# A new opening list, up to the eighth input unit, in a fused kernel of clustered attention and a SiLU expert

## The chip, the cores and the metric

One Trainium2 chip, one core of it. The metric is the time of one execution of the whole kernel on the device, in microseconds; lower is better. Before and after are compared as medians of several executions.

## What is computed

Attention over 4 batches, 8 heads, 768 positions and 64 dimensions. Each query and each key belongs to the one of 16 cluster centres of its head to which its normalised vector is closest, and a query sees only keys of its own cluster. A feed-forward layer with SiLU follows on all 3072 tokens (512 to 2048 to 512).

```python
q_assign = np.argmax(np.einsum('bhsd,hcd->bhsc', q_n, c_n), axis=-1)
k_assign = np.argmax(np.einsum('bhsd,hcd->bhsc', k_n, c_n), axis=-1)
mask = q_assign[:, :, :, None] == k_assign[:, :, None, :]
scores = np.where(mask, scale * np.matmul(q, k.transpose(0, 1, 3, 2)), -1e9)
attn = np.exp(scores - scores.max(-1, keepdims=True))
x = np.matmul(attn / attn.sum(-1, keepdims=True), v)      # (B, H, S, D) -> (B*S, H*D)
h = x @ w_in
return (h * (1.0 / (1.0 + np.exp(-h)))) @ w_out
```

## The kernel before

A **job** brings the queries and keys of one head from memory to the form in which they are multiplied. `load` fetches float32 rows, `hi` and `lo` split them into two float16 halves (scaled by 128), a transpose turns them into `ab` tiles with the 64 dimensions on partitions: on TensorE (`tr`, with `ev` to copy the result out of its bank) in the opening, by DMA (`xpose`) later. `logits_n` multiplies the tiles with the normalised centres (`stk`), `mx_n` and `ge_n` on VectorE make a one-hot code of the largest, and the code is written into 16 further partitions of the same `ab` tile. A match of codes then adds the same large number to a score, so that the exponential of a score without a match vanishes.

The code gets there by one of two ways. With `ct_mm`, `ct_q` and `ct_k`, nine transposes on TensorE put it where it belongs in a bank, and one ScalarE and two VectorE copies bring it from there into `ab`. With `cd_mm` and `cd_ev`, two matmuls and one copy make a tile `cd`, and a DMA on SP's queue moves it. Jobs of batches 2 and 3 use a DMA transpose and a move on GpSimd's queue.

For the first batch, jobs `k0` to `k7` hold a head's keys and the first half of its queries, and jobs `x0` and `x1` the second half of the queries of four heads each. Jobs `h8` to `h31` are the later batches' heads.

Work on TensorE comes in units. There are 192 **score units** (`qk_mm`: two matmuls of 384 columns for one half of the queries of a head and two key blocks), three for each head and half: units 0 to 23 are the first half of batch 0, units 24 to 35 the second half of its heads 0 to 3, which need `x0`'s codes. `exp` on ScalarE turns each into a tile `P`. Two banks hold scores, so score u waits for exp u-2. `pv` multiplies a pair of heads' `P` with the values (36 matmuls of 65 columns), `norm` divides by the row sums on VectorE, and `xn_t` with `xn_ev`, or the DMA transpose `xn_d`, turn the result into `xt`. An **input unit** (`unit_a`, 4 matmuls of 384 columns) multiplies `xt` with 128 columns of `w_in`; tanh on ScalarE and the gate on VectorE follow. An **output part** (`part_b`, 4 matmuls of 512 columns) multiplies with `w_out`.

Four further banks (0 to 3) hold everything else; an operation of the opening names its banks.

The order of work is fixed in the program in two ways. The **opening** is a list written out by hand or by a search (`plan`, line 650): each word is an operation with its index, an engine letter (A, D, P) or its banks, and each engine takes its own pieces in the order of the list. Words: `hi`/`lo`/`tr`/`ev` as above, `L` logits, `mx`, `ge`, `cm` and `ce` for `cd_mm` and `cd_ev`, `ct`, `ctq`, `ctk`; `x...` the same for jobs x0 and x1; `vl` and `v` load and cast values, `w` loads expert weights (0 to 3 and 4 to 7 are the two halves of `w_in`), `qk`, `ex`, `pa` `pb` `pc` or `px` `py` the parts of a `pv`, `nm`, `pt`, `pe` its normalisation, transpose and eviction; `a` and `e` begin and end an input unit; `r` loads a later job; `j` is filler work on TensorE.

Behind the list, from line 678, a **scheduler** in the program orders everything else: it keeps a model clock of each engine (lengths in us, such as 0.325 for a score unit), lets each engine take the piece that is ready with the best rank, and for TensorE (`options`, line 850) a score unit goes first when it is due (`PACE0`, `PACE`, line 859). Steps of a job get dates in score units (`p`, line 778), and `lanes` holds each engine's pieces with a lateness that orders them (`add`, line 694). None of this runs on the chip; it only decides the order in which instructions are issued. The list ends with unit 24 scored and three input units (`FIRST`, line 682; `range(3)`, line 793).

Of the kernel before, what the change touches and what calls it, by code (L numbers as in the profile page):

```python
# [28 lines left out]
@with_exitstack  # L29
def kernel(  # L30
# [10 lines left out]
    nc = tc.nc  # L41
# [118 lines left out]
    def logits_n(job, bk=None, w=HC, ns=None):  # L160
        ab = abs_[job.name]
        if job.name not in psNs:
            psNs[job.name] = bank("psN", n=bk)
        psN = psNs[job.name]
        m = (job.n + 1) // 2
        L = psN[:, 0 : 2 * w * m].rearrange("p (h c m) -> p h c m", h=2, m=m)
        for n in ns or range(2 * m):
            i = min(n, job.n - 1)
            for x in range(0, 2 * HC, w):
                nc.tensor.matmul(  # L170
                    L[:, n % 2, :, n // 2], ab[:, i, :], stk[:, job.groups[i // 3][0], x : x + w],
                    start=(x == 0), stop=(x + w == 2 * HC),
                )
        Ls[job.name] = L

# [3 lines left out]
    def lsum(job, last=True):  # L179
        m, P = job.n // 2, Ls[job.name]  # L180
        L = mp.tile([128, 2, HC, 6], f32, name="L", bufs=2)
        nc.vector.tensor_reduce(  # L182
            out=L[:, :, :, 0:m], in_=P.rearrange("p h (n c) m -> p h c m n", n=2), axis=AX.X, op=ALU.add
        )
        if last:
            done(psNs.pop(job.name))
        Ls[job.name] = L[:, :, :, 0:m]

    def ohv(job):
        m = (job.n + 1) // 2  # L190
        if job.late:
            return ohd[nn[job.name] % 3][:, :, 0 : HC * m].rearrange("p h (c m) -> p h c m", m=m)
        return ohm[nn[job.name] % 3][:, 0 : 2 * HC * m].rearrange("p (h c m) -> p h c m", h=2, m=m)

    def mx_n(job):
        m = (job.n + 1) // 2
        mx = mxn[job.name] = mp.tile([128, 12], f32, name="mxn", bufs=3)
        nc.vector.tensor_reduce(
            out=mx[:, 0 : 2 * m].rearrange("p (h m) -> p h m", h=2), in_=Ls[job.name].rearrange("p h c m -> p h m c"),
            axis=AX.X, op=ALU.max,  # L200
        )

    def ge_n(job):
        m = (job.n + 1) // 2
        nn[job.name] = len(nn)
        mx = mxn.pop(job.name)[:, 0 : 2 * m].rearrange("p (h m) -> p h m", h=2)
        nc.vector.tensor_tensor(  # L207
            out=ohv(job), in0=Ls.pop(job.name), in1=mx.unsqueeze(2).to_broadcast([128, 2, HC, m]), op=ALU.is_ge
        )
# [43 lines left out]
    def ct_mm(job, banks):  # L253
        for part, lo_, n, bk in (("q", 6, 3, banks[0]), ("k", 0, 6, banks[1])):
            pC = psCs[job.name, part] = bank("pC", f16, bk)
            for m in range(lo_, lo_ + n):
                x = 128 * (m - lo_)
                nc.tensor.transpose(pC[64 : 64 + HC, x : x + 128], ohv(job)[:, m % 2, :, m // 2], ident)
        psNs.pop(job.name)
# [297 lines left out]
    def first(op, n, eng, banks):  # L557
# [22 lines left out]
        elif op == "L":  # L580
            logits_n(job, banks[0])
        elif op == "mx":
# [79 lines left out]
    """.split()  # L662
    for word in plan:
        name, *rest = word.split(".")
# [16 lines left out]
    free.append(3)  # L681
    FIRST = 24
    PACE0, PACE = 1.3, 1.40
    HOLD = 6
# [27 lines left out]
    def date(s, f):  # L712
        dates.setdefault(s, []).append(f)

    code_at, tensor_todo = {}, []

    def chain(job, b):
# [7 lines left out]
        def turned(t):  # L725
            add("SP", t, 1.65, lambda: xpose(job), lambda t: tensor_todo.append((lands(t, 2.45) + (5.0 if b == 3 else 2.2 if b == 2 else 1.8), 0.35, lambda: logits_1(job), sums)))

# [48 lines left out]
    for i in range(H, B * H):  # L776
        b, h = divmod(i, H)
        p = int((32 + 3.2 * h, 64+5.2*h, 106+5.2*h)[b - 1]) | 1
        job = jobs[i]
        if i > H + 3:  # L780
            date(max(FIRST, p - (8 + min(h, 4) if b == 1 else 12)), lambda t, job=job: add("SP", t, 1.25, lambda: load(job), lambda t: got(job, t)))
        if i >= H + 2:
# [6 lines left out]

    exp_at = {u: 0.0 for u in range(FIRST - 1)}  # L790
    exp_at[FIRST - 1] = 0.0
    exp_at[FIRST] = 0.9
    x_at, gate_at = {}, {(0, 0, fb): 0.0 for fb in range(3)}
    pv_next = 4
    qa, qb = [(0, 0, fb) for fb in range(3, NFB)], []
    x_at[0, 0] = 0.0
    turn, po_on = 0, None
    unit = FIRST + 1

    def by_dma(n):  # L800
        return 8 <= n < 8 * B - 1

    def norm_piece(n, t):
        b, c, i = n // 8, n // 4 % 2, n // 8 * H + 2 * (n % 4)

        def ready(t):
            if n % 4 == 3:
                x_at[b, c] = t
                if n < 8 * B - 1:
# [40 lines left out]
    def options(t):  # L850
# [26 lines left out]
    def tensor_piece(o):  # L877
        nonlocal unit, pv_next, turn
        rank, r, length, what = o
        if what == "qk":  # L880
# [124 lines left out]
```

## Time and profile before

| | |
|---|---|
| median of 3 runs | 305.55 us (304.91 to 306.67) |
| the profiled execution | 306.13 us |
| its span | 304.4 us |
| TensorE busy | 297.6 us, 98% of the span |
| ScalarE busy | 213.3 us |
| VectorE busy | 202.1 us |
| GpSimd busy | 70.4 us |
| moved by DMA | 44.00 MB |

The span is the time between the first and the last event of the profiled execution. The page's slices give each engine's busy share in 40 equal parts of the span (7.6 us each), in tenths. A busy time is a union of the intervals in which an instruction is under way: short matmuls overlap each other, and so a stretch can count as busy although more would fit into it. In the lines of groups the columns are: source line, engine, operation, what is written from what, shapes, count; then busy us and the mean ns of one; then idle time of the engine ahead of them.

### The profile page before, as it was taken

What the parts mean: (1) busy time and instruction counts of PE and PEld (TensorE: products, weight loads), DVE (VectorE), ACT (ScalarE), POOL (GpSimd) and SP (SyncE); (2) the same over time, 40 slices, a digit from 0 to 9 for tenths busy, and PEclk for the clock granted to TensorE, in tenths of its full rate; (3) what the DMA queues carried; (4) which work ended last, traced back from release to release, by engine and by line L of the source; (5) the groups of instructions that cost most, each with busy time, mean ns of one, the idle gap of its engine ahead of it and who ended that gap; (6) DMA issues with size and microseconds to landing.
All of it is one profiled execution on the core that took longest, in us unless ns stands there. A gap on an engine that the chain in (4) does not pass through costs nothing.

```text
span 304.4 us, 7844 instructions
## 1 busy us (share of the span) xinstructions
PE 297.6 (98%) x3152; PEld 188.2 (62%) x3152; DVE 202.1 (66%) x431; ACT 213.3 (70%) x344; POOL 70.4 (23%) x130
## 2 busy tenths in 40 slices
PE   7899999999999999999999999999999999999996
PEld 3777856666666566665666566656665566655544
DVE  5997759888997669966679548873553235424542
ACT  5899979665887569965787658966996569752420
POOL 2987510111310332353222243212100000000000
PEclk9999999999999999999999999999999999999999
DMA  6989899999975799687998978552101110011012
GB/s 212 245 215 204 137 254 233 198 293 216 246 141 129 169 239 169 159 188 173 209 212 143 250 170 167 127 116 71 28 16 47 53 66 15 15 47 57 14 60 78
DMA packets 74419, 44.00 MB, mean 145 GB/s; under 512 B 54704, under 2 KB 69392, under 8 KB 74384
## 3 DMA queue, kind: packets, MB, share of 16 engines
q1 hardware_dynamic: 69296, 35.09, 49.1%
q0 software_dynamic: 4800, 8.13, 14.5%
q8 instruction: 24, 0.39, 0.5%
q10 hardware_dynamic: 288, 0.30, 0.3%
q14 instruction: 11, 0.09, 0.1%
HBM read 27.30 MB, written 6.29 MB: 110 GB/s over the span
## 4 chain that ended last, share of the span: by engine, by line
PE 87%; DMA 5%; ACT 3%; DVE 3%; issue 1%; SPq 1%; DVEq 0%
PE po L463 26%; PE ph L405 24%; PE pS L338 19%; PE pO L355 10%; PE psN L170 3%; DMA ab<-cd 2%; ACT P L343 2%; PE phs L443 2%; DMA raw<-in_k_dram 1%; PE po L969 1%; DMA vn<-in_v_dram 1%; DVE hl L122 1%; SPq L102 1%; PE pTk L145 0%; ACT ab L262 0%
## 5 line engine op out<-in xcount | busy, mean ns | idle before, releaser
L343 ACT ACTIVATE P<-pS 128x768 f16<-128x768 f32 x192 | 153.5, 816 | 53.4 <-PE pS L338 53.1
L338 PE MATMUL pS<-ab 128*128 128x384 f16 x384 | 91.4, 326 | 0.7 <-DMA ab<-cd 0.3
L405 PE MATMUL ph<-xt,win_s 128*128 128x384 f16 x480 | 91.0, 326 | 0.3 <-DVE gt L428 0.3
L463 PE MATMUL po<-wout_s,gt 128*128 128x512 f16 x368 | 91.0, 379 | 0.0
L428 DVE SCALAR_TENSOR_TENSOR gt<-tn,ph 128x384 f16<-128x384 f32 x120 | 63.0, 550 | 22.5 <-ACT tn L425 21.7
L425 ACT ACTIVATE tn<-ph 128x384 f32<-128x384 f32 x120 | 58.7, 504 | 9.8 <-PE ph L405 8.6
L405 PEld LDWEIGHTS <-win_s 128*128 128x128 f16 x480 | 46.1, 98 | 30.2 <-issue 0.9
L463 PEld LDWEIGHTS <-gt 128*128 128x128 f16 x368 | 35.4, 98 | 34.6
L338 PEld LDWEIGHTS <-ab 128*128 128x128 f16 x384 | 34.5, 98 | 26.3 <-issue 1.6
L355 PEld LDWEIGHTS <-P 128*128 128x128 f16 x1152 | 39.4, 97 | 4.0
L355 PE MATMUL pO<-vt,P 128*128 128x65 f16 x1152 | 41.0, 193 | 0.0
L470 DVE TENSOR_SCALAR ot<-po 128x512 f32<-128x512 f32 x23 | 15.9, 690 | 31.6 <-PE po L463 31.5
L122 DVE SCALAR_TENSOR_TENSOR hl<-raw,hl 128x768 f16<-128x768 f32 (+3 forms) x35 | 32.3, 926 | 0.9 <-ACT hl L113 0.3
L285 POOL CAST vt<-vn 128x384 f16<-128x384 f32 x32 | 17.6, 554 | 43.7 <-DMA vn<-in_v_dram 40.4
L227 POOL DMA_DIRECT2D ab<-cdt x16 | 9.1, 566 | 55.1 <-PE pS L338 19.4
L170 PEld LDWEIGHTS <-ab 128*128 128x128 f16 x472 | 17.4, 97 | 4.1
L182 DVE TENSOR_REDUCE L<-psN 128x192 f32<-128x384 f32 x26 | 14.3, 551 | 7.0 <-PE psN L170 6.9
L214 POOL TENSOR_SCALAR od<-od 128x96 f16<-128x96 f16 x16 | 9.8, 615 | 38.7 <-DVE od L207 38.6
L367 DVE TENSOR_TENSOR xn<-pO,zr 128x384 f16<-128x384 f32 x32 | 17.8, 558 | 1.1
L365 DVE RECIPROCAL zr<-pO 128x6 f32<-128x6 f32 x32 | 6.2, 193 | 18.6 <-PE pO L355 18.4
L170 PE MATMUL psN<-stk,ab 128*128 128x32 f16 (+1 forms) x472 | 18.4, 187 | 0.0
L117 DVE TENSOR_SCALAR hl<-raw 128x768 f16<-128x768 f32 x24 | 13.6, 567 | 0.7 <-DMA raw<-in_k_dram 0.7
(75 smaller groups left out, 162.9 us busy)
## 6 DMA issues: line engine op xcount, KB each, us to landing
raw<-in_k_dram SPq DMA_DIRECT2D x31, 192.0 KB, 3.7
out_dram<-ot SPq DMA_DIRECT2D x23, 256.0 KB, 2.2
raw<-in_q_dram SPq DMA_DIRECT2D x24, 192.0 KB, 3.6
vn<-in_v_dram SPq DMA_DIRECT2D x16, 192.0 KB, 4.4
vn<-in_v_dram POOLq DMA_DIRECT2D x16, 192.0 KB, 3.5
win_s<-in_moe_w_in_dram POOLq DMA_DIRECT2D x8, 256.0 KB, 6.3
wout_s<-in_moe_w_out_dram POOLq DMA_DIRECT2D x4, 512.0 KB, 10.6
raw<-in_q_dram SPq DMA_DIRECT2D x2, 384.0 KB, 5.0
```

The costliest lines, as they stand in the source:

```text
L122: nc.vector.scalar_tensor_tensor(out=hl[:, s, 1, :], in0=raws[job.name][:, s, :], scalar=QS, in1=hl[:, s, 0, :], op0=ALU.mult, op1=ALU.sub ...
L170: nc.tensor.matmul(L[:, n % 2, :, n // 2], ab[:, i, :], stk[:, job.groups[i // 3][0], x : x + w], start=(x == 0), stop=(x + w == 2 * HC),)
L285: nc.gpsimd.tensor_copy(vt[:, :, 0:D], vns.pop(i))
L338: nc.tensor.matmul(pS[:, e, 0:HALF], abs_[kj.name][:, kn, :], rhs, start=True, stop=True)
L343: nc.scalar.activation(out=P, in_=pst.pop(u)[:, :, 0:HALF], func=AF.Exp, bias=0.0, scale=ESC)
L355: nc.tensor.matmul(o[:, (2 * t + h) * VW : (2 * t + h + 1) * VW], Ps[i + h, c, j // 2][:, j % 2, ts(t, 128)], vtb[(i + h) % 13][:, j, 0:VW ...
L367: nc.vector.tensor_tensor(out=xn, in0=ov[:, :, 0:D], in1=zr.unsqueeze(2).to_broadcast([128, 2 * NM, D]), op=ALU.mult)
L405: nc.tensor.matmul(ph[:, 0:HALF], win_s[:, r, ts(fb, 128)], xts[b, c][:, r, :], start=(r == 0), stop=(r == NR - 1))
L425: nc.scalar.activation(out=tn, in_=ph[:, 0:HALF], func=AF.Tanh, bias=0.0, scale=0.5)
L428: nc.vector.scalar_tensor_tensor(out=gt[:, fb, :], in0=tn, scalar=1.0, in1=ph[:, 0:HALF], op0=ALU.add, op1=ALU.mult)
L463: nc.tensor.matmul(po, gts[b, c][:, fc, ts(t, 128)], wout_s[:, fc, :], start=(fc == 0), stop=(fc == NFB - 1))
L470: nc.vector.tensor_scalar(out=ot, in0=po, scalar1=0.5, scalar2=None, op0=ALU.mult)
```

## The change

A new list takes the place of the old one. It scores units 0 to 26 (before 0 to 24) and holds eight input units (before three); at its end stand the ends of two of them and six whole ones, with only one exponential and loads between. Heads 0 and 3 get their codes by `ct` (before heads 0, 1, 3, 4, 6 and 7), heads 1, 2, 4, 5, 6 and 7 by `cm` and `ce` (before heads 2 and 5). GpSimd splits four of the heads (3, 5, 7, 6; before 3, 5, 7). Jobs with `ct` use a flat layout (`flat`: nine code columns in one row, not two halves of five), so their logits are nine tiles and not ten. Head 7's logits are made 32 wide and summed by `ls`; the other heads' stay 16 wide in two accumulating matmuls.

In the scheduler, the number of scores and input units in the list is counted (`listed_s`, `listed_e`); the pace of the score units follows the stock of input and output work instead of a fixed pace; pair 11 is transposed by TensorE instead of by DMA; the dates of batch 2 move slightly; DMA loads get a lateness of 3, and so does the DMA transpose of batches 2 and 3.

```diff
@@ class Job @@
+        self.halves, self.m = 2, (self.n + 1) // 2
+    def flat(self):
+        self.halves, self.m = 1, self.n
...
@@ logits_n @@
-        m = (job.n + 1) // 2
-        L = psN[:, 0 : 2 * w * m].rearrange("p (h c m) -> p h c m", h=2, m=m)
-        for n in ns or range(2 * m):
+        g, m = job.halves, job.m
+        L = psN[:, 0 : g * w * m].rearrange("p (h c m) -> p h c m", h=g, m=m)
+        for n in ns or range(g * m):
...
@@ first @@
         elif op == "L":
-            logits_n(job, banks[0])
+            logits_n(job, banks[0], 2 * HC if eng else HC)
+        elif op == "ls":
+            lsum(job, False)
...
     plan = """
-        hk0 hq0 lk0 hi1.A cn0 j3.0 c5.01 lq0 hi2.A vl1 stk tk0.2 xr0 kad tq0.3 lo1 evq0.A hi3.P evk0.D tr1.01 evq1.A
-        hi4.A lo2 L0.2 evk1.D mx0 ge0 tr2.31 lo3 evq2.A ct0.02 ctk0 L1.1 lo4 evk2.A L2.3 ctq0 hi6.A tr3.02 evk3.D mx1
-        evq3.A qk0 mx2 ge1 ge2 qk1 w0 tr4.02 evq4.D ex0 qk2 cm2 hi5.P ct1.12 lo5 evk4.A ce2.A L3.0 ctq1 w1 hi7.P ex1
-        xh0.P vl0 ctk1 tr5.31 v1 ex2 qk3 mx3 evk5.D ge3 xr1 evq5.D L4.2 vl3 qk4 ex3 lo6 ct3.30 ex4 mx4 qk5 ctq3 L5.1
-        v0 ex5 ctk3 w2 mx5 vl2 ge5 ge4 qk6 tr6.30 qk7 evk6.D cm5 w3 vl5 w4 ce5.D xh1.P ex6 vl7 qk8 xl0 evq6.A ex7 ex8
-        ct4.23 pa0.0 ctq4 qk9 L6.1 w5 ex9 qk10 pb0 vl4 qk11 v3 pc0 ex10 lo7 ctk4 tr7.23 ex11 evq7.A qk12 ex12 mx6 qk13
-        ge6 nm0 v5 evk7.D pt0.0 ct6.13 qk14 xp0.2 xl1 pe0.A ex13 xu0.D ex14 ctk6 L7.0 qk15 w6 ctq6 xp1.2 qk16 mx7
-        xq0.3 ge7 v2 ex15 xu1.D ex16 ct7.10 qk17 xw0.D xL0.2 xM0 vl6 xs0 qk18 pa1.3 ex17 pb1 xm0 ex18 ctk7 v4 ctq7
-        qk19 qk20 pc1 w7 ex19 xg0 pa2.1 xc0 qk21 xq1.0 v7 ex20 qk22 ex21 xw1.A pb2 v6 xe0.D pc2 vl9 nm1 xL1.2 qk23 xM1
-        nm2 xs1 pt1.3 xm1 px3.0 xg1 ex22 ex23 pt2.1 vl8 w8 py3 w9 r8 pe1.A pe2.A w10 xc1 r9 nm3 a0.3 xe1.D w11 pt3.1
-        a1.0 r10 pe3.D e1 e0 e2.2 qk24 ex24 r11
+        hk0 hq0 hi1.A lk0 cn0 lq0 lo1 tk0.0 hi2.A evk0.D j3.1 c5.12 kad tq0.3 lo2 evq0.A tr1.23 stk vl4 L0.0 vl0
+        evq1.A evk1.D mx0 ge0 hi4.A tr2.13 evq2.A L1.2 hi3.P ct0.03 lo4 mx1 ge1 xr0 cm1 ctk0 hi5.P evk2.A lo5 ctq0
+        tr4.10 ce1.A qk0 hi7.P evk4.A lo3 L2.3 evq4.A tr5.21 mx2 evk5.D ge2 qk1 ex0 qk2 evq5.A w0 lo7 L4.0 vl1 ex1 mx4
+        cm2 tr3.12 ex2 ce2.A xr1 qk3 evq3.D evk3.A qk4 hi6.P tr7.32 ge4 lo6 cm4 L3.1 evq7.D xh0.P ex3 qk5 vl2 evk7.D
+        ce4.A v4 mx3 w1 ex4 tr6.20 evk6.D ex5 L5.3 ge3 mx5 vl5 qk6 v1 evq6.A ct3.21 vl3 ge5 qk7 cm5 L6.0 xl0 ctk3 ex6
+        ctq3 qk8 ce5.A L7.S.2 xq0.3 mx6 ge6 w2 ls7 xp0.1 xw0.D v0 xh1.P ex7 cm6 v2 v5 qk9 ex8 ce6.A qk10 ex9 pa0.3 mx7
+        ge7 pb0 vl6 xu0.D xl1 qk11 xL0.0 ex10 cm7 vl7 qk12 v3 ex11 xM0 ce7.D xs0 w3 pc0 v7 qk13 r8 xp1.1 ex12 qk14 xm0
+        ex13 xu1.D ex14 w4 xq1.2 qk15 xg0 v6 nm0 pa1.1 qk16 xw1.D xc0 pt0.3 ex15 xe0.D ex16 qk17 ex17 xL1.2 w5 pb1
+        qk18 vl8 ex18 xM1 qk19 pe0.D pc1 qk20 nm1 vl9 xs1 pa2.0 ex19 ex20 qk21 pb2 qk22 ex21 pc2 xm1 xg1 ex22 nm2 w6
+        qk23 px3.3 pt1.1 pe1.D ex23 pt2.0 xc1 py3 qk24 pe2.D w7 r9 xe1.A r10 nm3 ex24 qk25 a0.1 pt3.0 w8 qk26 a1.2
+        pe3.D ex25 w9 e0 e1 w10 e6.3 r11 e4.0 ex26 e2.1 e3.2 e5.3 w11 e7.0
     """.split()
+    for word in plan:
+        if word[:2] == "ct" and word[2].isdigit():
+            jobs[int(word[2])].flat()
+    listed_e = sum(w[0] == "e" and w[1].isdigit() for w in plan)
+    listed_s = sum(w[:2] == "ex" for w in plan)
...
-    FIRST = 24
-    PACE0, PACE = 1.3, 1.40
+    FIRST = listed_s
+    PACE, LEAST, GAIN = 1.40, 12, .03
...
-        p = int((32 + 3.2 * h, 64+5.2*h, 106+5.2*h)[b - 1]) | 1
+        p = int((32 + 3.2 * h, 67+5.0*h, 106+5.2*h)[b - 1]) | 1
...
     def by_dma(n):
-        return 8 <= n < 8 * B - 1
+        return 8 <= n < 8 * B - 1 and n != 11
...
@@ options @@
-                due = t >= PACE0 * min(unit - FIRST - 1, 24) + PACE * max(unit - FIRST - 25, 0)
+                stock = 1.302 * len(qa) + 0.863 * len(qb) + 20.8 * (unit // 24 - released)
+                due = t >= scored + min(max(PACE + GAIN * (stock - LEAST - 0.867 * (24 - unit % 24)), 0.8), 2.2)
...
@@ tensor_piece, behind a score unit @@
+            scored = max(clock["PE"] - 0.325, scored + 0.8)
```

More of the change, by code (lines that the diff above doesn't have):

```diff
@@ L170, in logits_n @@
                 nc.tensor.matmul(
-                    L[:, n % 2, :, n // 2], ab[:, i, :], stk[:, job.groups[i // 3][0], x : x + w],
+                    L[:, n % g, :, n // g], ab[:, i, :], stk[:, job.groups[i // 3][0], x : x + w],
                     start=(x == 0), stop=(x + w == 2 * HC),
@@ L179, in lsum @@
     def lsum(job, last=True):
-        m, P = job.n // 2, Ls[job.name]
-        L = mp.tile([128, 2, HC, 6], f32, name="L", bufs=2)
+        g, m, P = job.halves, job.m, Ls[job.name]
+        L = mp.tile([128, 12 * HC], f32, name="L", bufs=2)[:, 0 : g * HC * m].rearrange("p (h c m) -> p h c m", h=g, m=m)
         nc.vector.tensor_reduce(
-            out=L[:, :, :, 0:m], in_=P.rearrange("p h (n c) m -> p h c m n", n=2), axis=AX.X, op=ALU.add
+            out=L, in_=P.rearrange("p h (n c) m -> p h c m n", n=2), axis=AX.X, op=ALU.add
         )
@@ L257, in ct_mm @@
                 x = 128 * (m - lo_)
-                nc.tensor.transpose(pC[64 : 64 + HC, x : x + 128], ohv(job)[:, m % 2, :, m // 2], ident)
+                nc.tensor.transpose(pC[64 : 64 + HC, x : x + 128], ohv(job)[:, m % job.halves, :, m // job.halves], ident)
         psNs.pop(job.name)
@@ L712, in date @@
     def date(s, f):
[L713 removed]
+        dates.setdefault(max(s, FIRST), []).append(f)
     code_at, tensor_todo = {}, []
@@ L787 @@
         date(60, lambda t, od=od: add("POOL", t, 0.3, lambda: nc.gpsimd.memset(od, 0.0)))
[L790 to L793, printed above, removed]
+    exp_at = {u: 0.0 for u in range(FIRST)}
+    exp_at[FIRST - 1] = 0.9
+    x_at, gate_at = {}, {(0, 0, fb): 0.0 for fb in range(listed_e)}
     pv_next = 4
-    qa, qb = [(0, 0, fb) for fb in range(3, NFB)], []
+    qa, qb = [(0, 0, fb) for fb in range(listed_e, NFB)], []
     x_at[0, 0] = 0.0
     turn, po_on = 0, None
-    unit = FIRST + 1
+    released, scored = 1, -1.0
+    unit = FIRST
     def by_dma(n):
-        return 8 <= n < 8 * B - 1
+        return 8 <= n < 8 * B - 1 and n != 11
     def norm_piece(n, t):
@@ L806, in ready @@
         def ready(t):
+            nonlocal released
             if n % 4 == 3:
+                released += 1
                 x_at[b, c] = t
@@ L877, in tensor_piece @@
     def tensor_piece(o):
-        nonlocal unit, pv_next, turn
+        nonlocal unit, pv_next, turn, scored
         rank, r, length, what = o
```

20 lines of the change are left out of this document (10 added, 10 removed).

## The prediction

> **What bounds the kernel now.** The profiled execution took 306.13 us in all with a span of 304.4, so 1.73 us lie around the span; the median of the three runs is 305.55, or 0.58 below the profiled one. I read the page's busy times and slices first, then TensorE by stretches.
>
> ```profile
> PE 297.6 (98%) x3152; PEld 188.2 (62%) x3152; DVE 202.1 (66%) x431; ACT 213.3 (70%) x344; POOL 70.4 (23%) x130
> ...
> PE   7899999999999999999999999999999999999996
> ...
> PEclk9999999999999999999999999999999999999999
> ...
> 41.00:291.00 250.00, 249.50 (x2497) 155.26 (x2496) 165.33 (x330) 179.30 (x288) 45.44 (x91) 1.00 0.63 139
> ```
>
> The reader is to see that TensorE is the bound from 41 us on: 249.50 busy of 250.00 at a granted clock of 1.00. Nothing is to be had there but by giving TensorE fewer instructions. The busy share flatters the opening, because a short matmul counts with its whole latency. So I work with pitches, the distance at which equal matmuls follow each other, from the order of time on TensorE:
>
> ```profile
> 10.28 1.17 PE L170 MATMUL psN<-stk,ab 128*128 128x16 f16 x40
> 11.29 0.49 PE L145 MATMUL pTk<-ident,hl 128*128 128x128 f16 x6
> ...
> 11.90 0.81 PE L338 MATMUL pS<-ab 128*128 128x384 f16 x4
> ...
> 17.47 0.68 PE L258 MATMUL pC<-ident,om 128*16 128x128 f16 x9
> 18.08 0.50 PE L338 MATMUL pS<-ab 128*128 128x384 f16 x2
> ...
> 30.13 0.51 PE L170 MATMUL psN<-stk,ab 128*128 128x32 f16 x12
> 30.48 0.49 PE L338 MATMUL pS<-ab 128*128 128x384 f16 x2
> ...
> 35.16 0.49 PE L338 MATMUL pS<-ab 128*128 128x384 f16 x2
> ...
> 40.48 0.81 PE L338 MATMUL pS<-ab 128*128 128x384 f16 x4 [0.32 <-DMA ab<-cd]
> ...
> 43.72 1.46 PE L405 MATMUL ph<-xt,win_s 128*128 128x384 f16 x8
> 45.02 0.49 PE L338 MATMUL pS<-ab 128*128 128x384 f16 x2
> ...
> 48.11 1.09 PE pO L355 x36
> ```
>
> The first two numbers of a line are its start and length. Pitches: a 16-wide logit 1.01/40 = 0.025 us, a 32-wide one 0.35/12 = 0.029, an input matmul 1.30/8 = 0.1625, the same for a score matmul (equal width), a value matmul 1.09/36 = 0.030 (last line, from the chain of waits). For transposes I take the length less one matmul's own 0.22 us: (0.49 - 0.22)/5 = 0.054 for a tile, (0.68 - 0.22)/8 = 0.0575 for a code tile (0.61/9 = 0.068 if the gap behind counts too).
>
> The starts give a milestone that both kernels pass with the same work done: eight input units finished and score units 0 to 27 issued. Counting score pairs, unit 0 starts at 11.90, unit 23 at 35.16, unit 28 at 45.02. **So the milestone of before is 45.02 us**, and the question is when the new list gets there.
>
> **The change part by part.** First the matmul count, by the order of the built programs against these groups:
>
> ```profile
> L170 PE MATMUL psN<-stk,ab 128*128 128x32 f16 x312 | 13.3, 193 | 0.0
> L170 PE MATMUL psN<-stk,ab 128*128 128x16 f16 x160 | 5.1, 176 | 0.0
> L258 PE MATMUL pC<-ident,om 128*16 128x128 f16 x54 | 4.1, 221 | 0.4 <-DVE om L207 0.4
> L236 PE MATMUL psN<-ident,om 128*80 128x128 f16 x4 | 0.6, 226 | 0.0
> ```
>
> Code transposes go from 54 to 18 (-36 x 0.0575 = -2.07 us), the code matmuls of heads from 4 to 12 (+8 x 0.054 = +0.43), 16-wide logits from 160 to 136 (-0.60), 32-wide ones from 312 to 322 (+0.29), transposes of normalised outputs from 27 to 30 (+0.16, since pair 11 no longer goes by DMA). Sum -1.8 us. All but the last lie ahead of the milestone. They are worth 1.8 only if TensorE is what the opening waits for, and until unit 23 it isn't: ScalarE is.
>
> ```profile
> 12.49 0.81 ACT L343 ACTIVATE P<-pS 128x768 f16<-128x768 f32 x1
> 13.63 0.81 ACT L154 ACTIVATE ab<-pTk 128x768 f16<-128x768 f16 x1 [0.34 <-PE pTk L145]
> 14.37 0.47 ACT L247 ACTIVATE cd<-psN,kadd 80x256 f16<-80x256 f32 x1
> 14.86 0.48 ACT L262 ACTIVATE ab<-pC 16x384 f16<-16x384 f16 x1
> 15.37 3.02 ACT L343 ACTIVATE P<-pS 128x768 f16<-128x768 f32 x4
> ...
> 20.31 0.50 ACT L154 ACTIVATE ab<-pTq 128x384 f16<-128x384 f16 x1
> 20.68 1.53 ACT L343 ACTIVATE P<-pS 128x768 f16<-128x768 f32 x2
> ...
> 35.15 1.54 ACT L343 ACTIVATE P<-pS 128x768 f16<-128x768 f32 x2
> ```
>
> From start to start: an exponential 3.02/4 = 0.755, a K eviction 0.74, a code copy out of the bank 0.49, a query code copy 0.51, a Q eviction 0.37. Before, exp 0 starts at 12.49 and exp 22 at 35.15, which is 22.66 us: 22 exponentials (16.61) and between them one K eviction (0.74), one bank copy (0.49), five query code copies (2.55), two Q evictions (0.74), and two pieces that the new list gives to VectorE, x1's 768-wide Q eviction and the first output pair's, taken like head evictions of their widths (0.74 + 0.37): together 22.24. ScalarE idled only about 0.4.
>
> *The start of the exponentials.* The new list puts head 1's maximum and comparison ahead of head 0's key codes on VectorE, and head 1's bank copy, head 4's K and Q evictions ahead of exp 0 on ScalarE:
>
> ```profile
> 8.94 0.31 DVE L198 TENSOR_REDUCE mxn<-psN 128x10 f32<-128x160 f32 x1
> 9.28 0.33 DVE L207 TENSOR_TENSOR om<-psN,mxn 128x160 f16<-128x160 f32 x1
> ...
> 11.04 0.62 DVE L269 TENSOR_SCALAR ab<-pC 16x256 f16<-16x256 f16 x2
> ```
>
> Key codes follow at 11.04 + 0.31 + 0.33, so unit 0 is scored near 11.90 + 0.6 = 12.5. On ScalarE the bank copy waits for that comparison and a short code matmul (11.7 + 0.3 = 12.0), ends at 12.5, then come 0.74 and 0.37 for head 4 with about 0.1 of hand-over: exp 0 at 13.7, 1.2 us later than before.
>
> *The stream behind it.* Until exp 22 the new order has on ScalarE 16.61 of exponentials, two Q evictions (0.74), one K eviction (0.74), four bank copies (1.96) and one query code copy (0.51): 20.56. With the same idle 0.4, exp 22 starts at 13.7 + 21.0 = 34.7, 0.45 earlier than before, and with it score unit 23.
>
> *From unit 23 to the milestone.* Now TensorE has work queued without a gap: five score units (10 x 0.1625), 32 input matmuls (5.2), 36 value matmuls (1.09), nine transposes (0.49), two code matmuls (0.11): 8.5 us, which ends at 43.2. Before, the same plus six logits (0.17) is 8.7 us and took 9.86; 1.2 us went into waits, one of them the 0.32 for x0's codes at 40.48. The new list has x0's code copy five scores earlier and only the last pair's transpose and eviction close to the input units, covered by units 25 and 26. I take no loss here; the bounds are 0 and the 1.2 of before.
>
> *What is added: waits for code transfers.* Heads 1, 4, 6 and 7 now send their codes through a DMA on SP's queue instead of copies on ScalarE and VectorE, as heads 2 and 5 did. Before shows these four in the opening, those of heads 2 and 5, x0 and x1: the issues of the first two and then each landing (us, last column), in order of time, with the stretches' DMA share (last but one column):
>
> ```profile
> 14.86 0.69 SPq L251 DMA_DIRECT2D ab<-cd  x1
> ...
> 20.92 0.58 SPq L251 DMA_DIRECT2D ab<-cd  x1
> ```
> ```profile
> ab<-cd SPq DMA_DIRECT2D x1, 40.0 KB, 2.6
> ...
> ab<-cd SPq DMA_DIRECT2D x1, 40.0 KB, 6.7
> ...
> ab<-cd SPq DMA_DIRECT2D x1, 48.0 KB, 6.7
> ...
> ab<-cd SPq DMA_DIRECT2D x1, 48.0 KB, 10.5
> ```
> ```profile
> 12.00:16.00 4.00, 3.62 (x57) 2.61 (x55) 3.86 (x12) 3.51 (x6) 3.44 (x2) 1.00 0.83 145
> 16.00:20.00 4.00, 3.82 (x69) 2.89 (x68) 3.67 (x11) 3.95 (x7) 3.04 (x6) 1.00 0.78 241
> 20.00:24.00 4.00, 3.85 (x68) 2.77 (x67) 3.70 (x9) 3.95 (x7) 3.56 (x2) 1.00 1.16 196
> ```
>
> The tightest is head 2. Its bank copy follows exp 2: 13.7 + 3 x 0.755 + 0.37 + 0.49 = 16.8, and the issue comes at once. Exp 6 could start at 16.8 + 0.74 + 0.755 + 0.49 + 1.51 + 0.37 = 20.7, so unit 6 wants the codes by 20.15. A landing in 2.6 us costs nothing, one in 6.7 lands at 23.5 and costs 3.4. The issue is two us behind the 2.6 row and four ahead of the 6.7 one, so I go a third of the way: 4.0 us, a wait of 0.7. Queued behind the waiting score on TensorE are later heads' logits and transposes, so ScalarE, VectorE and the later code copies all move with it; later heads then have their slack enlarged and I charge them nothing more. Head 1, issued near 12.5 and wanted near 17, is safe up to 4.5 us.
>
> By the Trainium skill, "DMA: Bandwidth & Descriptors", section on the anatomy of one DMA, a transfer costs about 2.0 us plus its bytes over 436e3 per us (fitted there on the GpSimd path), an estimate of 2.1 for 40 KB. By that no code is late and the sum is the first rival below. The trace agrees only where the DMA share was 0.83 (2.6); at 1.16 it shows 6.7.
>
> *GpSimd* takes one more split (head 6) and sends the expert weights later; the weights' second half is first wanted behind the milestone, so I put this at nothing, covered by the eight first-half input units.
>
> **Sum.** Milestone 43.2 + 0.7 = 43.9 against 45.02: -1.1. Behind it the two programs have equal counts but for the three transposes, +0.16. The new pacing rule and dates only permute that work: from a job's logits to the first score that uses it the shortest stretch holds 9.8 us of TensorE work against 10.1 before, and from the last pair of batch 1's first half to its first input unit 2.4. Before lost 0.5 in that stage; I take the same. So -0.95 against the profiled time, and against the median 305.55 - 0.95 = **304.6 us**.
>
> **The rivals.** (1) *All codes land in time*: milestone 43.2, -1.8 + 0.16, 303.9 us. For it the 2.6 row, against it the 6.7 one. (2) *Slower: x0's codes come late at unit 24.* Its copy is listed ahead of exp 16, which ScalarE reaches near 29.7; I put the issue at 30. Unit 24 stands on TensorE behind the last value matmuls, near 36.95, and every input unit of the list stands behind it. With 6.7 the codes land at 36.7 and cost nothing; with the 10.5 that x1's took, they land at 40.5 and all stops for 3.55 us. With head 2's 0.7 that makes a milestone of 47.4, +2.4 + 0.16, or about 308.1 us; alone it is 307.4. It decides from a landing of about 9 us on. For it: the list loads batch 1's data ahead of that transfer. Against: 6.7 in the comparable place. (3) *The opening's gain is given back in the rest*, by the new pace letting ScalarE or a bank run late by 1 us or so: 305.6. Against it, the distances above.
>
> **How the numbers follow.** Forecast 0.4, (1) 0.3, (2) 0.2, (3) 0.1. What a measurement can tell from no change is about 0.5%, 1.5 us, so faster means below 304.0. Of the forecast case a third ends below that by a landing nearer 2.6, of (1) about 0.8: faster 0.37. Same takes 0.6 of the forecast, the rest of (1), most of (3): 0.39. Slower 0.24 is (2) and a tenth of the forecast. Range: down to 302.4, rival (1) with ScalarE's 0.4, the 0.5 of the rest and half a us of the runs' spread gained as well; up to 307.3, almost the second rival.
>
> **What would show it.** In the new profile unit 0 at 12.5 and exp 0 at 13.7; exp 22 near 35.4 with a ScalarE idle near 20 us released by a score that waited for a code transfer; unit 24 with no DMA wait; the eighth input unit's end near 43.9. Wrong would be: exp 0 below 13 or above 14.5, a DMA wait over 2 us at any score, or a TensorE idle over 1 us behind the milestone, where late weights would stop the first input units of the second half.

## The result and the profile after

| | before | after |
|---|---|---|
| median of 20 runs each | 306.36 us (304.91 to 308.69) | 305.33 us (303.88 to 306.92) |
| ratio, with its 95% interval | | 0.9951 [0.9931, 0.9970] |
| the profiled execution | 306.13 us | 304.68 us |
| its span | 304.4 us | 302.8 us |

The change makes the kernel about half a per cent faster, 1.5 us by the ratio and 1.0 us by the medians; the ratio's interval lies wholly below 1. Here and below, "before" and "after" also name the two kernels. From the page of the changed kernel, its busy times and TensorE's slices:

```profile
PE 294.3 (97%) x3113; PEld 186.3 (62%) x3113; DVE 200.6 (66%) x427; ACT 211.2 (70%) x341; POOL 69.1 (23%) x131
...
PE   7899989999999999999999999999999999999995
```

TensorE still sets the time. It has less to do, and two of the groups that the prediction counted on have the predicted counts (groups by form; the number behind x is the count, then busy us and mean ns):

```profile
L382 PE MATMUL px<-ident,xn 128*128 128x128 f16 x30 | 3.2, 219 | 0.0
L263 PE MATMUL pC<-ident,om 128*16 128x128 f16 x18 | 1.4, 222 | 0.0
```

Next, TensorE in order of time (start, length), the places that the prediction named:

```profile
11.89 0.49 PE L343 MATMUL pS<-ab 128*128 128x384 f16 x2
...
27.35 0.48 PE L343 MATMUL pS<-ab 128*128 128x384 f16 x2
...
32.82 0.48 PE L343 MATMUL pS<-ab 128*128 128x384 f16 x2
...
34.70 0.81 PE L343 MATMUL pS<-ab 128*128 128x384 f16 x4
...
36.47 4.87 PE L410 MATMUL ph<-xt,win_s 128*128 128x384 f16 x29
41.18 0.49 PE L343 MATMUL pS<-ab 128*128 128x384 f16 x2
42.52 0.81 PE L410 MATMUL ph<-xt,win_s 128*128 128x384 f16 x4 [0.84 <-DVE gt L433]
```

These are score units 0, 16 and 23, unit 24 with 25, the last 29 matmuls of the eight input units, unit 27, and the first input unit behind the list. The milestone (eight input units done, units 0 to 27 issued) is the end of unit 27 at its pitch, 41.18 + 2 x 0.1625 = 41.50 us. Before it was 45.02, so the opening won 3.52 us, not the 1.1 of the forecast. The last row shows what came right behind: no work for TensorE until 42.52, and in its brackets the profile names what ended the wait, a gate on VectorE. That is 1.02 us lost again.

From there to the end the two kernels differ little. The chain of waits of after ends with a copy into an output tile at

```profile
299.56 0.23 DVE ot L992
```

and that of before the same copy at

```profile
301.67 0.23 DVE ot L975
```

which is 2.11 us later. So -3.52 + 1.02 + 0.16 (three transposes more) leaves 0.23 of loss in everything between. The span shrank by 1.6 only. The outputs are not the cause: the issues of the last three began 2.12 us earlier (298.71 against 300.83), and the last of them, 32 KB, landed 1.5 us behind its issue in both profiles. The missing 0.5 lies behind that landing, in the closing instructions of the program; why, no run here tells.

### The profile page after: what moved, and what is told of

Same layout as the page of the kernel before. It is cut to its first block, busy times and chain, and to the rows that moved or that the text cites. A ratio compares the mean times of both kernels' runs of the same rounds, so it can differ in the third digit from the quotient of the medians.

```text
span 302.8 us, 7783 instructions
## 1 busy us (share of the span) xinstructions
PE 294.3 (97%) x3113; PEld 186.3 (62%) x3113; DVE 200.6 (66%) x427; ACT 211.2 (70%) x341; POOL 69.1 (23%) x131
## 3 DMA queue, kind: packets, MB, share of 16 engines
q1 hardware_dynamic: 69264, 35.16, 50.8%
## 4 chain that ended last, share of the span: by engine, by line
PE 87%; ACT 4%; DVE 4%; DMA 2%; SPq 1%; issue 1%; DVEq 0%; ACTq 0%
PE ph L410 25%; PE po L468 25%; PE pS L343 19%; PE pO L360 11%; PE psN L175 3%; ACT P L348 3%; PE phs L448 2%; DVE hl L127 1%; PE po L986 1%; DMA raw<-in_k_dram 1%; DMA xt<-xn 1%; SPq L107 1%; ACT ab L159 1%; PE px L382 0%; SPq L228 0%
## 5 line engine op out<-in xcount | busy, mean ns | idle before, releaser
L348 ACT ACTIVATE P<-pS 128x768 f16<-128x768 f32 x192 | 155.6, 821 | 55.1 <-PE pS L343 54.7
L343 PE MATMUL pS<-ab 128*128 128x384 f16 x384 | 93.2, 326 | 0.5 <-ACT P L348 0.4
L410 PE MATMUL ph<-xt,win_s 128*128 128x384 f16 x480 | 92.4, 326 | 1.2 <-DVE gt L433 0.8
L433 DVE SCALAR_TENSOR_TENSOR gt<-tn,ph 128x384 f16<-128x384 f32 x120 | 64.0, 549 | 23.7 <-ACT tn L430 23.1
L430 ACT ACTIVATE tn<-ph 128x384 f32<-128x384 f32 x120 | 60.1, 507 | 10.1 <-PE ph L410 8.1
L187 DVE TENSOR_REDUCE L<-psN 128x192 f32<-128x384 f32 (+1 forms) x27 | 14.9, 550 | 15.1 <-PE psN L175 15.0
```

Of the source, the lines that this page charges most:

```text
L343: nc.tensor.matmul(pS[:, e, 0:HALF], abs_[kj.name][:, kn, :], rhs, start=True, stop=True)
L348: nc.scalar.activation(out=P, in_=pst.pop(u)[:, :, 0:HALF], func=AF.Exp, bias=0.0, scale=ESC)
L410: nc.tensor.matmul(ph[:, 0:HALF], win_s[:, r, ts(fb, 128)], xts[b, c][:, r, :], start=(r == 0), stop=(r == NR - 1))
L430: nc.scalar.activation(out=tn, in_=ph[:, 0:HALF], func=AF.Tanh, bias=0.0, scale=0.5)
L433: nc.vector.scalar_tensor_tensor(out=gt[:, fb, :], in0=tn, scalar=1.0, in1=ph[:, 0:HALF], op0=ALU.add, op1=ALU.mult)
```

## The experiments

Three questions were open. Does the list alone bring the gain, with the new rules of the scheduler only permuting the rest, as the prediction said? Is the us behind the milestone the price of a bank? And what limited the opening, ScalarE or TensorE? The kernels were run in three groups, each on one chip beside 29 to 35 runs of the kernel before (medians 306.67, 307.20 and 306.96 us), and each ratio is to those.

### The new list under the old rules

```diff
-    PACE, LEAST, GAIN = 1.40, 12, .03
+    PACE0, PACE = 1.3, 1.40
...
-                due = t >= scored + min(max(PACE + GAIN * (stock - LEAST - 0.867 * (24 - unit % 24)), 0.8), 2.2)
+                due = t >= PACE0 * min(unit - FIRST, 24) + PACE * max(unit - FIRST - 24, 0)
...
-        return 8 <= n < 8 * B - 1 and n != 11
+        return 8 <= n < 8 * B - 1
```

Also the old dates of batch 2, and no lateness for loads and transposes.

> The new list with the old scheduler rules (fixed pace, old dates of batch 2, no lateness for loads and DMA transposes, pair 11 by DMA again). Theory A, the opening list brings all of the gain: the milestone (eighth input unit done, 28 scores issued) stays at 41.5 us, 3.5 ahead of before, and the time is within 0.7 us of the changed kernel's, ratio to before 0.994 to 0.997; three transposes fewer give back 0.16. Theory B, the scheduler's rules bring it: the ratio is 1.000 or above although the milestone is 41.5, with TensorE idle over 2 us behind it.

Measured: 308.45 us (12 runs), ratio 1.0073 [1.0040, 1.0106]. The milestone stood at 41.75 us, as early as in after, and yet the kernel is slower than before. Busy time by stretches, here the sums over 47 to 291 us (244 us; TensorE's busy time is behind PE), first of before, then of after, then of this kernel:

```profile
sum 244.00, PE 243.50 PEld 151.66 DVE 162.30 ACT 173.30 POOL 44.49; mean PE 81.17 PEld 50.55 DVE 54.10 ACT 57.77 POOL 14.83
```
```profile
sum 244.00, PE 243.09 PEld 150.85 DVE 162.63 ACT 171.48 POOL 43.87; mean PE 81.03 PEld 50.28 DVE 54.21 ACT 57.16 POOL 14.62
```
```profile
sum 244.00, PE 240.12 PEld 149.10 DVE 160.04 ACT 170.32 POOL 44.31; mean PE 80.04 PEld 49.70 DVE 53.35 ACT 56.77 POOL 14.77
```

TensorE is idle for 0.50 us in before, 0.91 in after and 3.88 here. The waits of TensorE name the places (us in total, times, longest):

```profile
PE psN L175 <- DMA ab<-hl: 1.7, 1, 1.7
PE px L382 <- DVE xn L372: 0.9, 1, 0.9
```

The longest, 1.66 us, is a job's logits at 133.63 that wait for its DMA transpose. SP's queue shows that transpose issued only at 128.17, with raw loads of a later job close behind:

```profile
128.17 1.44 SPq L136 DMA_TRANSPOSE ab<-hl  x1
129.66 0.87 SPq L107 DMA_DIRECT2D raw<-in_q_dram  x1
```

What follows: the list alone doesn't bring the gain. Its 3.27 us (41.75 against 45.02) are lost again between 47 and 200 us, where the old rules leave TensorE idle for 3.38 us more than in before. Another 1.00 goes at the hand-over, by the order of the free banks (below), and the last output copy stands at 303.63, 1.96 us later than in before.

### The old list under the new rules

The plan text of before in the changed kernel, with the flat layout for its `ct` heads.

> The old list with the new scheduler rules. Theory A: milestone near 45.0 as before, and the time equals before, ratio 0.999 to 1.003. Theory B: ratio 0.995 to 0.997 with the milestone at 45.0.

Measured: 306.32 us (12 runs), ratio 1.0016 [0.9986, 1.0045]. TensorE idles less in the rest than in before (0.06 us by the sum below against 0.50), but its unit 24 came at 40.71 us (before: 40.48), behind a wait of 0.7 for x0's codes.

```profile
sum 244.00, PE 243.94 PEld 152.04 DVE 163.81 ACT 173.04 POOL 46.36; mean PE 81.31 PEld 50.68 DVE 54.60 ACT 57.68 POOL 15.45
```

What follows: the rules alone bring nothing that can be told from no change. The gain needs both halves.

### The order of the free banks

The chain of waits of after, around the idle us (start, length, what):

```profile
41.38 0.50 ACT tn L430
...
41.91 0.57 DVE gt L433
...
42.52 0.81 PE ph L410 x4
```

The tanh and the gate are those of the list's last input unit, `e7.0`, and the matmuls that follow are the first input unit of the scheduler. It was given bank 0, the bank that `e7.0` had just filled. The list names its banks, so the scheduler's model has no release times for them and starts with all four free at 0.0, in the order 0, 1, 2, 3. Bank 1 (`e2.1`) was free first.

```diff
-    free.append(3)
+    free[:] = [1, 2, 3, 0]
```

This changes which bank the scheduled pieces use and leaves the order of instructions on every engine as it was.

> The changed kernel, but the first input unit behind the list takes bank 1 (freed by the list's third input unit from the end of its gates) in place of bank 0, which the list's last unit frees last. Theory: the 1.0 us in which TensorE stood still at 41.5 us for the gate of the list's last unit goes, units of TensorE's order are unchanged, so the time falls by 0.8 to 1.1 us against the changed kernel, ratio to before near 0.992. Rival: the wait only moves to the next units, since gates follow each other at 0.5 us and ScalarE's exponentials are due then: gain below 0.3 us.

Measured: 304.10 us (12 runs), ratio 0.9949 [0.9917, 0.9981], span 301.2 us. TensorE in order of time:

```profile
41.25 0.49 PE L343 MATMUL pS<-ab 128*128 128x384 f16 x2
41.57 0.81 PE L410 MATMUL ph<-xt,win_s 128*128 128x384 f16 x4
```

The input unit follows the score at its pitch, 0.32 us, where after took 1.34. Beside it ran the changed kernel itself once more:

> The changed kernel itself, beside the others on the same chip: ratio to before 0.993 to 0.997 as measured, milestone at 41.5 us, a wait of about 1 us behind it for the gate of the list's last input unit.

Measured: 305.20 us (12 runs), ratio 0.9962 [0.9938, 0.9986]. The two medians, from one chip, are 1.1 us apart, as the trace says; the intervals of the ratios overlap, so that this us is shown by the trace and only supported by the times. This profile of the unchanged kernel also has a wait which the first one lacks, at unit 15, the first that needs head 5's codes:

```profile
28.23 0.50 PE L343 MATMUL pS<-ab 128*128 128x384 f16 x2 [1.40 <-DMA ab<-cd]
```

The landing of that transfer (40 KB, last column, us) in this profile, and in the first one of the same kernel:

```profile
ab<-cd SPq DMA_DIRECT2D x1, 40.0 KB, 6.9
```
```profile
ab<-cd SPq DMA_DIRECT2D x1, 40.0 KB, 4.5
```

The same instructions in the same order, and the two landings differ by 2.4 us.

### The rules one at a time

Only the old fixed pace in the changed kernel (the diff of the pace above):

> The changed kernel with the old fixed pace of score units alone (dates, lateness and pair 11 stay new). Theory A, the new pace is what the new list needs (the list ends with eight input units' gates as stock, which a pace that runs by the clock from zero doesn't see): the loss of 1.2% of the run with all old rules returns almost whole, ratio to before 1.003 to 1.007, TensorE idle over 3 us between 47 and 140 us. Theory B, it is the lateness of loads and transposes on SP's queue: ratio 0.995 to 0.998, at most 1 us more of idle.

Measured: 308.26 us (12 runs), ratio 1.0035 [0.9997, 1.0074]. Only the lateness of loads and transposes taken away:

```diff
-            add("SP", ..., lambda: xpose(job), ..., 0.0 if b == 1 else 3.0)
+            add("SP", ..., lambda: xpose(job), ...)
...
-        date(..., lambda t, job=job: add("SP", t, 1.25, lambda: load(job), lambda t: got(job, t), 3.0))
+        date(..., lambda t, job=job: add("SP", t, 1.25, lambda: load(job), lambda t: got(job, t)))
```

> The changed kernel without the new lateness of DMA loads and DMA transposes alone. Theory A: ratio 0.994 to 0.998, as the changed kernel. Theory B: ratio 1.002 to 1.007, with waits of TensorE for DMA transposes of later jobs (1.7 us in the run with all old rules).

Measured: 306.90 us (12 runs), ratio 0.9996 [0.9965, 1.0027], between the bands of the two theories. The sums over 47 to 291 us, first with the old pace, then without the lateness:

```profile
sum 244.00, PE 242.00 PEld 150.49 DVE 160.29 ACT 172.19 POOL 43.13; mean PE 80.67 PEld 50.16 DVE 53.43 ACT 57.40 POOL 14.38
```
```profile
sum 244.00, PE 240.87 PEld 149.79 DVE 160.70 ACT 170.37 POOL 44.71; mean PE 80.29 PEld 49.93 DVE 53.57 ACT 56.79 POOL 14.90
```

TensorE is idle for 2.00 and 3.13 us there, against 0.91 in after. With the old pace it waits above all for gates, without the lateness above all for transposes. From the waits of TensorE from 41 us on (the first row holds the 0.84 at the bank as well):

```profile
PE ph L410 <- DVE gt L433: 2.5, 4, 1.1
```
```profile
PE psN L175 <- DMA ab<-hl: 1.8, 2, 0.9
```

What follows: with the new list the pace carries part of the gain, and the lateness probably does. Against the 0.9951 and 0.9962 of the full change, the pace is worth about 0.8% and the lateness about 0.4%. The interval of the old pace lies above both intervals of the full change; that without the lateness overlaps them, so that its part rests on the waits for transposes in one profile. The sizes are rough: the profile of the old pace was 1.4 us faster than its median, that without lateness 1.3 us slower, so the two idle times don't rank them. The old pace's idle time between 47 and 140 us was smaller than expected, and its longest wait for a gate (1.07 us) stood at 152 us. Pair 11's way and the dates of batch 2 were not tried alone.

### What limits the opening

Four kernels add work that does nothing for the output; all have the bank order above. First four copies on ScalarE behind exponentials 10, 12, 14 and 16:

> The kernel with the new bank order and four useless copies of 384 columns on ScalarE behind exponentials 10, 12, 14 and 16 (about 0.37 us each, 1.5 in all). If ScalarE bounds the stretch from unit 9 to unit 23, score unit 23 and the milestone come 1.2 to 1.5 us later (milestone from 41.5 to 42.8 or more, without a wait for a code transfer). If TensorE bounds it, under 0.5.

Measured: 304.19 us (2 runs only), ratio 0.9895 [0.9842, 0.9948]. Unit 15 waited 0.84 us for head 5's codes in this profile, in the middle of the stretch to be measured, so that it decides nothing. Then TensorE, with the logits of head 6 taken twice, those of head 7 three times, and those of x0 twice, 20 + 20 + 12 = 52 matmuls more:

> The kernel with the new bank order and 52 logit matmuls repeated (head 6 once, head 7 twice, the first halves of x0 once each: 20 x 0.0255 + 32 x 0.029 = 1.4 us of TensorE work between 20 and 26 us). If ScalarE bounds the stretch, the milestone moves by less than 0.7 us, since TensorE stood still for about 0.8 there and the repeats fill that; if TensorE does, by 1.2 to 1.4.

```profile
19.81 0.50 PE L343 MATMUL pS<-ab 128*128 128x384 f16 x2
...
23.24 0.81 PE L343 MATMUL pS<-ab 128*128 128x384 f16 x4
...
37.24 0.81 PE L343 MATMUL pS<-ab 128*128 128x384 f16 x4 [1.10 <-DMA ab<-cd]
```

Measured: 305.66 us (8 runs), ratio 0.9940 [0.9910, 0.9970]. Unit 9 came 10.59 us behind exponential 0 (12.65 to 23.24); in the kernel with the bank order alone it was 9.24 (13.01 to 22.25). These 1.35 us don't decide anything, because without added work ahead of unit 9 the same distance runs from 9.13 to 10.36 over the profiles of the new list. The stretch from unit 7 to unit 9 does: it holds all the 1.09 us of work added ahead of unit 9, took 2.34 to 2.49 us in the eleven other profiles of the new list, and takes 23.24 - 19.81 = 3.43 here (the first two rows are units 7 and 9). That is 0.94 to 1.09 more: between units 7 and 9 TensorE has no room. From unit 9 to unit 23, 0.34 us of work cost 0.22 against the bank order alone, too little to be read beside the spread. The milestone at 44.04 includes a wait of 1.10 for x0's codes.

Next the stretch between units 16 and 23, with the bank order alone once more as the base:

> The new bank order again, beside the former on the same chip: ratio to before 0.990 to 0.996; milestone 41.5 us, or 1 to 1.5 later where the profiled execution has a wait for head 5's codes.

```profile
27.67 0.48 PE L343 MATMUL pS<-ab 128*128 128x384 f16 x2
...
33.13 0.48 PE L343 MATMUL pS<-ab 128*128 128x384 f16 x2
```

Measured: 304.50 us (12 runs), ratio 0.9928 [0.9895, 0.9961]; units 16 to 23 take 33.13 - 27.67 = 5.46 us, and 5.45 to 5.47 in all nine profiles of the new list without added work there, whether unit 15 had waited for codes or not. Four copies on ScalarE behind exponentials 16 to 19, each 0.41 us from start to start, 1.6 us in all:

```diff
-... ex15 xe0.D ex16 qk17 ex17 xL1.2 w5 pb1
-qk18 vl8 ex18 xM1 ... pa2.0 ex19 ex20 ...
+... ex15 xe0.D ex16 ad0 qk17 ex17 ad1 xL1.2 w5 pb1
+qk18 vl8 ex18 ad2 xM1 ... pa2.0 ex19 ad3 ex20 ...
```

> The new bank order, with four useless ScalarE copies (1.5 us in all) behind exponentials 16 to 19, where no code transfer was late. From score unit 16 to score unit 23 the new bank order took 5.46 us. If ScalarE bounds that stretch: 6.5 to 7.0. If TensorE does: 5.4 to 5.8.

```profile
28.22 0.48 PE L344 MATMUL pS<-ab 128*128 128x384 f16 x2
...
34.81 0.49 PE L344 MATMUL pS<-ab 128*128 128x384 f16 x2
```

Measured: 304.75 us (8 runs), ratio 0.9928 [0.9891, 0.9964]. The stretch takes 34.81 - 28.22 = 6.59 us, 1.13 more, and four of its scores wait 0.26 to 0.33 us for an exponential. And 36 matmuls on TensorE instead, x1's twelve logits four times instead of once, 36 x 0.029 = 1.04 us:

> The new bank order, with 36 logit matmuls of x1 repeated between exponential 17 and score unit 19 (36 x 0.029 = 1.04 us of TensorE work). From score unit 16 to 23, against 5.46: if ScalarE bounds the stretch, 5.5 to 5.8, if TensorE does, 6.2 to 6.5.

```profile
28.73 0.50 PE L343 MATMUL pS<-ab 128*128 128x384 f16 x2 [1.99 <-DMA ab<-cd]
29.43 0.49 PE L343 MATMUL pS<-ab 128*128 128x384 f16 x2
...
35.68 0.48 PE L343 MATMUL pS<-ab 128*128 128x384 f16 x2
```

Measured: 305.62 us (8 runs), ratio 0.9955 [0.9917, 0.9993]. The stretch takes 6.25 us, 0.79 more.

What follows: in this stretch 1.6 us on ScalarE cost 1.13 and 1.04 us on TensorE cost 0.79, about 70% and 75%. Neither engine alone is what the opening waits for; both stand close to their limit there, and between units 7 and 9 TensorE stands at it. Sums over the pitches fit that: of the 5.46 us, TensorE's work makes 4.70 and seven exponentials at 0.73 make 5.1. What fills the rest, such as the hand-over between the two engines at the two score banks, was not tested. Each kernel with added work has one profile only.

### An earlier code of head 5, by a later load

Since head 5's codes were late in several profiles, the load of values listed ahead of them was moved back, and its cast with it:

```diff
-... L5.3 ge3 mx5 vl5 qk6 ... ex7 cm6 v2 v5 qk9 ...
+... L5.3 ge3 mx5 qk6 ... ex7 cm6 v2 qk9 ...
...
-ge7 pb0 vl6 ... w3 pc0 v7 ...
+ge7 pb0 vl5 vl6 ... w3 pc0 v5 v7 ...
```

> The new bank order, and the load of head 5's values (192 KB) moved on SP's queue from just ahead of head 5's code transfer to behind head 6's; its cast on GpSimd stands behind head 3's. Theory: the code transfer of head 5, which took 3.7 to 6.9 us and in some executions stopped score unit 15 (0.7 to 1.4 us), takes about 1 us less, no DMA wait at unit 15, and the median is 0.3 to 0.8 us below that of the new bank order alone. Rival: the transfer is slow by all the loads under way then, and nothing changes beyond 0.2 us.

Measured: 304.79 us (12 runs), ratio 0.9911 [0.9880, 0.9941], no better than the bank order beside it (304.50 us). Head 5's codes landed in 5.9 us here and in 5.1 there, so the transfer didn't get faster. (In the profiles ahead of this one it took 4.5 to 6.9 us, not from 3.7 as the expectation says.) Unit 15 waited 0.24 us in this profile, and a long wait stood at the first input unit behind the list:

```profile
44.17 0.34 PE L410 MATMUL ph<-xt,win_s 128*128 128x384 f16 x1 [1.26 <-DMA win_s<-in_moe_w_in_dram]
```

GpSimd issues weights behind casts of values, and the casts wait for their loads. The last such issue of the second half, in this kernel and then in after:

```profile
31.60 1.59 POOL L487 DMA_DIRECT2D win_s<-in_moe_w_in_dram  x3
```
```profile
30.16 1.59 POOL L487 DMA_DIRECT2D win_s<-in_moe_w_in_dram  x3
```

It comes 1.44 us later: the loads moved back hold up a cast, and the weights behind it in GpSimd's order. These weights are close to late without this change too. In the profile of the bank order beside it the last of them landed at 42.51 us, and the first input unit behind the list took 1.07 us instead of 0.81 because its fourth matmul began only at 42.56. So with the banks in order, the weights can be the next thing that TensorE waits for there.

### All twelve

The milestone of before is 45.02 us and that of after 41.50. In the kernel with the old list and the new rules unit 28 comes ahead of the eighth input unit, so that its milestone can't be compared.

| kernel | median us | ratio [95%] | milestone us | code waits of the profile |
|---|---|---|---|---|
| new list, old rules | 308.45 | 1.0073 [1.0040, 1.0106] | 41.75 | 0.23 (unit 3) |
| old list, new rules | 306.32 | 1.0016 [0.9986, 1.0045] | not comparable | 0.7 (unit 24) |
| bank order | 304.10 | 0.9949 [0.9917, 0.9981] | 41.57 | none |
| after again | 305.20 | 0.9962 [0.9938, 0.9986] | 43.07 | 1.40 (unit 15) |
| old pace | 308.26 | 1.0035 [0.9997, 1.0074] | 41.98 | none |
| no lateness | 306.90 | 0.9996 [0.9965, 1.0027] | 42.30 | 0.66 (unit 15) |
| copies on ScalarE, early | 304.19 | 0.9895 [0.9842, 0.9948] | 42.30 | 0.84 (unit 15) |
| logits again, early | 305.66 | 0.9940 [0.9910, 0.9970] | 44.04 | 1.10 (unit 24) |
| later load | 304.79 | 0.9911 [0.9880, 0.9941] | 42.25 | 0.24 (unit 15) |
| bank order again | 304.50 | 0.9928 [0.9895, 0.9961] | 41.82 | 0.78 (unit 3) |
| copies on ScalarE, late | 304.75 | 0.9928 [0.9891, 0.9964] | 43.42 | 0.22 (unit 3) |
| logits again, late | 305.62 | 0.9955 [0.9917, 0.9993] | 44.37 | 1.99 (unit 15) |

The bank order is the version to keep: on two chips it ran at 0.9949 and 0.9928 of before, with medians of 304.10 and 304.50 us, and the trace shows what it takes away.

## Why the prediction was right, and where its steps were wrong

The forecast was 304.6 us, 0.95 below the profile of before. Measured were 305.33, 1.03 below by the medians, and 1.45 below by the profiles. The sign, the size and the range held. Two large errors of opposite sign are in that: the opening won 3.52 us where the forecast had 1.1, and 1.75 us were lost where it had nothing (1.02 at the hand-over, 0.23 behind it, 0.5 at the program's end). That the sum came so close is in good part luck.

**The matmul count** was right. Taking every group of TensorE at the pitches of the prediction, after holds 1.80 us less work than before (287.75 against 289.55): 1.96 less ahead of the milestone and the three transposes, 0.16, more behind it.

**"Until unit 23 it isn't: ScalarE is"** was wrong, and with it the judgement that this work counts for little. The prediction had unit 23 0.25 us later than before (0.45 won, 0.7 lost to codes); it came 2.34 earlier (32.82 against 35.16). Up to the milestone TensorE had 33.37 us of work by pitches against 35.33, and besides it stood still or ran slower than its pitches for 6.95 us against 8.51, from its first matmul at 1.18 on. So, as bookkeeping, the 3.52 us are 1.96 of work and 1.56 of waiting. The kernels with added work on either engine support this reading: both are close to their limit, so less work on TensorE and less on ScalarE pay together. What each part of the new list is worth was not tried alone. The windows of the prediction already had TensorE at 3.82 and 3.85 of 4.00 beside ScalarE's 3.95, and those of after have both near the full 4.00 (the first number behind the stretch's length is TensorE's busy time, the fourth ScalarE's):

```profile
20.00:24.00 4.00, 4.00 (x80) 3.19 (x78) 3.87 (x11) 3.95 (x8) 2.58 (x2) 1.00 1.09 244
24.00:28.00 4.00, 4.00 (x67) 3.28 (x66) 3.93 (x9) 3.96 (x7) 1.55 (x3) 1.00 0.67 173
```

**ScalarE's stream** was the right chain with pieces too long. Its order of time in after:

```profile
13.02 0.81 ACT L348 ACTIVATE P<-pS 128x768 f16<-128x768 f32 x1
...
15.47 0.50 ACT L252 ACTIVATE cd<-psN,kadd 80x256 f16<-80x256 f32 x1
15.82 0.84 ACT L159 ACTIVATE ab<-pTk 128x768 f16<-128x768 f16 x1
...
22.48 0.47 ACT L252 ACTIVATE cd<-psN,kadd 80x256 f16<-80x256 f32 x1
22.84 8.18 ACT L348 ACTIVATE P<-pS 128x768 f16<-128x768 f32 x11
31.25 2.96 ACT L348 ACTIVATE P<-pS 128x768 f16<-128x768 f32 x4 [0.24 <-ACT P L348]
```

A bank copy takes 0.35 or 0.36 from start to start (15.47 to 15.82, 22.48 to 22.84), where the prediction took 0.49 from one whose follower had a reason of its own to start late; four of them make 0.5. The 22 exponentials, from all such starts, took 16.05 us against 16.61, 0.73 each. Exponential 0 came at 13.02 against 13.7. With the 0.7 of late codes that this profile didn't have, these are the main parts of the difference: exponential 22 started at 32.70 (two places into the last row, 31.25 + 2 x 0.725) and not at 35.4. **From unit 23 to the milestone** it was 8.68 us against 8.5, a hit.

**Unit 0 "near 12.5"** was 11.89, as before. The two more steps ahead of head 0's key codes did come on VectorE, but the codes started only 0.18 later (11.22 against 11.04), for the split in front of them was shorter (1.21 us against 1.49). Before, unit 0 had stood behind three transposes that began at 11.72, not behind the codes. This is the order of time on VectorE in after:

```profile
9.39 1.21 DVE L127 SCALAR_TENSOR_TENSOR hl<-raw,hl 128x576 f16<-128x576 f32 x1
...
11.22 0.63 DVE L274 TENSOR_SCALAR ab<-pC 16x256 f16<-16x256 f16 x2
```

**Late codes** were near in size by luck and wrong in place. The prediction charged 0.7 us to head 2 and called head 1 safe. Over the twelve profiles with the new list the waits sum to 7.46, or 0.62 each, but they stood at head 5 (unit 15), head 1 (unit 3) and once at x0 (unit 24), never at head 2. Head 2's codes landed in 2.4 to 3.2 us, not 4.0; head 1's were wanted near 15.3 us, not near 17; and 5.13 of the 7.46 stood at head 5, a later head that the prediction charged with nothing. The first rival's premise, that all codes land in time, held in three of the twelve profiles, that of after among them. The second rival, x0's codes late by 3.55, showed at 1.10 at most. By the Trainium skill, "DMA: Bandwidth & Descriptors", section on the anatomy of one DMA, the 40 KB come to an estimate of 2.1 us (fitted there on the GpSimd path; these go by SP's queue). The transfers of 40 KB in the openings of all profiles took 2.2 to 7.5 us, so here the measurement decides against that figure.

Of **the signs** that the prediction named, unit 24 without a DMA wait came true in after. Exponential 0 below 13, a sign of being wrong, came in ten of the twelve profiles; the eighth input unit ended at 41.18, not near 43.9; and the idle time of over 1 us behind the milestone, the other sign of being wrong, came for a bank and not for weights.

**"The new pacing rule and dates only permute that work"** is the step that failed outright. It weighed distances between steps and took the rest as unchanged under any rule. The list without the rules is slower than before by 0.73%, and taking one of two rules out of the change costs some 0.4% (not clear of noise) or 0.8%. The likely reason, argued and not shown, is that the fixed pace counts from the list's end without regard to how much work is in stock, and the new list ends with eight input units already spent. The third rival, a bank late by a us, did come true with 1.02 us, though not in the rest but at the hand-over; it had a chance of 0.1 and no place in the sum. "Late weights would stop the first input units" was named as a danger; after doesn't have it, the bank order has 0.25 of it in one of two profiles, and the later load 1.26.

## What to carry to other kernels

Two engines can each be near their limit in one stage, and then a saving on either is worth having. A share of busy time near one on the engine that you call free is a warning; work added to each engine in turn, over a stretch whose time repeats, is the test. When a list written by hand ends and a scheduler takes over, look at the state that it starts from: here its banks, in the wrong order, cost a us that one line gave back. And a change that brings a new list and new rules has to be weighed as one: here the list alone was slower, and the rules alone could not be told from no change.

## What the hardware showed unexpectedly

The landing of a small transfer from one place in SBUF to another varies by more than the stage can hide: head 5's 40 KB took 4.5 and 6.9 us in two profiles of the same program on the same queue, up to 7.5 in another kernel with the same list up to there, and head 2's 40 KB only 2.4 to 3.2. A copy out of a bank of 80 x 256 is 0.47 to 0.52 us long on ScalarE, but the next instruction starts 0.35 to 0.38 us behind its start; for this copy a sum over lengths, or over a row whose follower waits, is about a third too large.
